# Batch 0's norms: rows summed on VectorE before one norm matmul a group, odd rows as two groups of 96 by 3

## The chip, the cores and the metric

The kernel runs on one core of a Trainium2 chip. The metric is device time in microseconds (us), median of several executions. One further execution was profiled; all lines shown of the profile are of that one.

## The reference

There are two parts, one after the other, over B = 4 batches of N = 6208 rows and C = 256 channels.

The first is an attention over channels. With q, k, v of shape (B, N, C):

```python
qn = q / (norm(q, axis=1) + 1e-6)      # one norm a batch and channel, over all N rows
kn = k / (norm(k, axis=1) + 1e-6)
s = kn.T @ qn / tau                    # (C, C) per batch
a = softmax(s, axis=-1)
x = v @ a                              # (N, C)
```

The second is a channel-mix network on x, with `x_prev` the row above:

```python
xk = mu_k * x + (1 - mu_k) * x_prev ;  xr = mu_r * x + (1 - mu_r) * x_prev
k = relu(xk @ w_k)                     # 256 -> 1024
out = sigmoid(xr @ w_r) * ((k * k) @ w_v)
```

So nothing of the output can be computed until all rows of a batch's q and k have been read. The sum of q times k gives the 256 by 256 matrix, and the sums of their squares over the rows give 512 norms.

## The kernel before

All instructions are written in the order in which each engine runs them; the schedule is fixed by the order of the calls. Semaphores make an instruction wait for the tiles it needs, and what stands behind it on the same engine waits with it.

**Batch 0** is loaded first, on its own. Rows come in groups: in the kernel before group 0 has the 64 odd rows (64 partitions, one row each), groups 1 to 11 have 128 partitions with four consecutive rows each, and groups 12 and 13 have 128 by 2. They are taken in the order 1, 2, 0, 3, ... 13. For each group the loop at lines 517 to 531 does this:

- `group_load` (line 121) issues two loads in float32 on SyncE's queue, one of q and one of k. At most eight loads of the queue are under way; a further one waits for the semaphore of an earlier one, and for its buffer.
- `group_cast` (line 138) makes bf16 copies of q and k on VectorE (line 142), and the squares of both, in bf16, on ScalarE (line 144).
- `unit_matmul` (line 171) adds the group's rows to the covariance in PSUM: two matmuls with 256 columns for each of the group's row slots (line 182), so eight for a group with four.
- `group_norms` (line 191) sums the squares over the partitions: a matmul with a block of ones as weights, one for each row slot, into one 32-partition strip of PSUM a slot (line 197). That is for groups up to `DIRECT` = 9.
- For the groups after it, 10 to 13, `norms_direct` (line 203) adds the sums into the final layout, with channels on partitions: four matmuls of one column for each row slot (line 210).
- `keep_warm(3)` (line 508) issues three matmuls whose result nobody reads, in groups 5 to 9.

At group 10 (`DIRECT + 1`), after its casts and before its matmuls, `copies` moves the strips from PSUM to SBUF on VectorE (line 224) and `gather` turns them into the final layout with four float32 matmuls (line 231; eight passes in the trace).

At group 11 a small copy on GpSimd (line 530) waits for the group's first cast. It holds back the loads on GpSimd's queue (v, the weights, batch 1's q and k) until then.

**The softmax of batch 0** then runs in a chain: `roots` on ScalarE (line 248, after a load of the function table), `evac` (264), `invert` on VectorE (256 to 259), `turn` on TensorE (271), `exp` (279), `weigh` (293), and `x_first` (364), with unread matmuls between them.

**The rest** is a loop over 48 blocks of 512 rows plus a last block, with the network of one block, the attention product of a later one and the covariance of batches 1 to 3 put between each other by hand. The v tiles must be transposed; from block 4 on a DMA on SyncE's queue does it (line 321), with the stores of the results (line 474) in the same queue. Norms of batches 1 to 3 are summed in another way (lines 163 to 169), which stays.

Of the kernel before, what the change touches and what calls it, by code (L numbers as in the profile page):

```python
# [14 lines left out]
OP = mybir.AluOpType  # L15
# [3 lines left out]
def kernel(  # L19
# [13 lines left out]
    nc = tc.nc  # L33
    B, N, C = q.shape
    D = C
    DF = moe_w_k.shape[1]
    P = 128
    M = 512
    S = M // P
    assert C == 256 and DF == 1024  # L40
    NB = N // M
    L = N - NB * M
# [16 lines left out]
    ones = const.tile([P, P], BF16, name="ones")  # L59
# [4 lines left out]
    thirty2 = const.tile([P, P], F32, name="thirty2")  # L64
# [21 lines left out]
    cov = {}  # L86
    bank = {}
# [2 lines left out]
    sums = {}  # L90
    now = [0]
    groups = {}
    summed = set()
    DIRECT = NB - 3

    def sizes(b):
        return [1] + [S] * (NB - 1) + ([S // 2] * 2 if b == 0 else [S])

    def order(b):
        g = list(range(len(sizes(b))))  # L100
        return [1, 2, 0] + g[3:]

    def rows_of(b, g):
        return (P if g else L), sizes(b)[g]

    def qk_src(t, b, g):
        if g == 0:
            return t[b, NB * M:, :].rearrange("(p j) c -> p j c", j=1)
        r = P * sum(sizes(b)[1:g])
        n = sizes(b)[g]  # L110
        return t[b, r:r + P * n, :].rearrange("(p j) c -> p j c", p=P)

    def apart(b, g):
        return b == 1 and g > 0
# [1 line left out]
    def rows_at(qk, b, g, i):  # L116
        if apart(b, g):
            return qk.rearrange("p s i c -> p (s i c)").rearrange("p (i s c) -> p i s c", i=2, s=S)[:, i]
        return qk[:, :, i]

    def group_load(b, g):
        rows, n = rows_of(b, g)
        qk = pq.tile([P, S, 2, C], BF16, name="qk", tag="qk", bufs=5)
        groups[b, g] = (qk,)
        if b == 0:
            qk2 = pq.tile([P, S, 2, C], BF16, name="qk2", tag="qk2", bufs=4)
            groups[b, g] += (qk2,)
            t_f = []
            for i, t in enumerate((q, k)):
                f = pq.tile([P, S, C], F32, name=f"f{i}", tag=f"f{i}", bufs=6)  # L130
                nc.sync.dma_start(f[:rows, :n], qk_src(t, b, g))
                t_f.append(f)
            groups[b, g] += tuple(t_f)
        else:
            for i, t in enumerate((q, k)):
                nc.gpsimd.dma_start(rows_at(qk, b, g, i)[:rows, :n], qk_src(t, b, g))  # L136

    def group_cast(b, g):
        rows, n = rows_of(b, g)
        qk, qk2, *t_f = groups[b, g]  # L140
        for i in range(2):
            nc.vector.tensor_copy(qk[:rows, :n, i, :], t_f[i][:rows, :n])  # L142
        for i in range(2):
            nc.scalar.activation(qk2[:rows, :n, i, :], t_f[i][:rows, :n], AF.Square)  # L144

    def unit_square(b, g, s):

        rows, n = rows_of(b, g)
        if s % 2:
            return  # L150
        qk = groups[b, g][0]
        if n == 1:
            t = pq.tile([P, 1, 2 * C], BF16, name="sq", tag="sq1", bufs=2)
            sums[b, "left"] = t
        elif (g, s) == (1, 0):
            t = pn.tile([P, 2, 2 * C], F32, name="acc", tag="acc", bufs=2)
            sums[b] = t
        else:
            t = pq.tile([P, 2, 2 * C], F32, name="sq2", tag=f"f{s // 2}", bufs=6)
            adds.append((now[0] + 2, b, t))  # L160
        if apart(b, g):
            for i in range(2):
                nc.scalar.activation(t[:rows, :, i * C:(i + 1) * C], rows_at(qk, b, g, i)[:rows, s:s + 2], AF.Square)
        else:
            nc.scalar.activation(t[:rows], qk[:rows, s:s + min(n, 2)].rearrange("p s i c -> p s (i c)"), AF.Square)  # L165
# [5 lines left out]
    def unit_matmul(b, g, s):  # L171
        rows, n = rows_of(b, g)
        t0 = g == order(b)[0] and s == 0
        te = g == len(sizes(b)) - 1 and s == n - 1
        if t0:

            cov[b] = (ps.tile([P, 2, C], F32, name="s_ps", tag="s_ps" if b else "vr_ps", bufs=1 if b else 2),
                      ps.tile([P, 2 * C], F32, name="ssq_ps", tag="vr_ps", bufs=2) if b == 0 else None)
        s_ps = cov[b][0] if b or g <= DIRECT else cov["s"]
        qk = groups[b, g][0]  # L180
        for ih in range(2):
            nc.tensor.matmul(s_ps[:, ih, :], rows_at(qk, b, g, 0)[:rows, s, ih * P:(ih + 1) * P],  # L182
                             rows_at(qk, b, g, 1)[:rows, s, :], start=t0 and ih == 0, stop=te,
                             skip_group_check=True)
        if s == n - 1 and b == 0:
            if g > DIRECT:
                norms_direct(g)
            else:
                group_norms(b, g)

    def group_norms(b, g):

        rows, n = rows_of(b, g)
        ssq_ps = cov[b][1]
        qk2 = groups[b, g][1]
        for u in range(n):
            nc.tensor.matmul(ssq_ps[32 * u:32 * (u + 1)], ones[:rows, :32],
                             qk2[:rows, u].rearrange("p i c -> p (i c)"),
                             start=u not in summed, stop=g == DIRECT, tile_position=(0, 32 * u),
                             skip_group_check=True)  # L200
            summed.add(u)

    def norms_direct(g):

        rows, n = rows_of(0, g)
        qk2 = groups[0, g][1]
        for u in range(n):
            flat = qk2[:rows, u].rearrange("p i c -> p (i c)")
            for i in range(4):
                nc.tensor.matmul(bank[0][:, C + i:C + i + 1], flat[:, i * P:(i + 1) * P], ones[:rows, 0:1],  # L210
                                 start=False, stop=g == len(sizes(0)) - 1 and u == n - 1, skip_group_check=True)

    def softmax_pieces(b):

        s_ps, ssq_ps = cov.pop(b) if b else cov[b]
# [5 lines left out]
        rk = rn[:, 2:4]  # L221
        def copies():
            cov["ssq"] = pn.tile([P, 2 * C], F32, name="ssq", tag="ssq", bufs=1)
            nc.vector.tensor_copy(cov["ssq"], ssq_ps)

        def gather():

            cov["s"] = cov[b][0]
            bank[b] = ps.tile([P, 2 * C], F32, name="bank", tag="xT_ps", bufs=2)
            for i in range(4):  # L230
                nc.tensor.matmul(bank[b][:, C + i:C + i + 1], cov["ssq"][:, i * P:(i + 1) * P], thirty2[:, 0:1],
                                 start=i == 0, stop=False, skip_group_check=True)

        def fold():
# [60 lines left out]
        if b == 0:  # L295
            return [copies, gather, roots, evac, invert, turn, exp, weigh_dve]
# [14 lines left out]
    def v_load(i):  # L311
        b, t = blocks[i]
        v_bf = p2.tile([P, S, C], BF16, name="v_bf", tag="v_bf", bufs=6)
        nc.gpsimd.dma_start(v_bf, v[b, t * M:(t + 1) * M, :].rearrange("(s p) c -> p s c", p=P))  # L314
        st[i, "v"] = v_bf
# [8 lines left out]
    def v_transpose_pe(i, evac):  # L324

        v_bf = st.pop((i, "v"))
        vT_ps = ps.tile([P, S, 2, P], BF16, name="vT_ps", tag="kT_ps", bufs=3)
        for s in range(S):
            for h in range(2):
                nc.tensor.transpose(vT_ps[:, s, h], v_bf[:, s, h * P:(h + 1) * P], ident)  # L330

        def go():
            vT = p2.tile([P, S, 2, P], BF16, name="vT", tag="vT", bufs=5)
            evac(vT, vT_ps)
            st[i, "vT"] = vT
        return go
# [171 lines left out]
    def keep_warm(n):  # L508

        junk_ps = ps.tile([P, M], F32, name="junk_ps", tag="kT_ps", bufs=3)  # L510
        for _ in range(n):
            nc.tensor.matmul(junk_ps, ones, fill, start=True, stop=True)

    mu_ps = ps.tile([P, 4], F32, name="mu_ps", tag="xT_ps", bufs=2)
    nc.tensor.transpose(mu_ps, mu_rows, ident_f[:4, :4])
    nc.vector.tensor_copy(mu_t, mu_ps)
    for g in order(0):
        group_load(0, g)
        group_cast(0, g)
        if g == DIRECT + 1:  # L520
            copies, gather, roots, evac, invert, turn, exp, weigh = softmax_pieces(0)
            copies()
            gather()
        for s in range(sizes(0)[g]):
            unit_matmul(0, g, s)
        if 5 <= g <= DIRECT:
            keep_warm(3)
        if g == NB - 1:

            nc.gpsimd.tensor_copy(gate, groups[0, g][0][:, 0, 0, 0:1])  # L530
            v_load(0)

    units = [(b, g, s) for b in range(1, B) for g in order(b) for s in range(sizes(b)[g])]
    loads = [(b, g) for b in range(1, B) for g in order(b)]
# [52 lines left out]
    go = v_transpose_pe(0, nc.vector.tensor_copy)  # L587
# [18 lines left out]
    for i in range(-2, NBLK - 1):  # L606
        for j in range(8):
# [26 lines left out]
            if i + 2 < NBLK:  # L634
                n = i + 2
# [78 lines left out]
```

## Time and profile before

| what | value |
|---|---|
| median of 6 runs | 513.28 us (512.68 to 514.12) |
| the profiled execution | time 514.12 us, span of its instructions 512.3 us |
| TensorE matmuls busy | 492.1 us, 96% of the span, 3524 instructions |
| VectorE busy | 440.9 us, 86% |
| ScalarE busy | 449.8 us, 88% |
| GpSimd busy | 99.9 us, 19% |
| 0 to 12.8 us: TensorE, VectorE, ScalarE busy | 4.81, 5.11, 7.13 us; 315 GB/s moved |
| 12.8 to 25.6 us | 11.79, 6.94, 10.57 us; 410 GB/s |
| 25.6 to 33 us | 5.45 of 7.4, 4.74, 6.16 us; 402 GB/s |
| 38 to 45 us | 5.94 of 7, 5.23, 3.89 us; 192 GB/s |
| 200 to 300 us | 99.94, 94.04, 94.26 us; 165 GB/s |

Busy time of a matmul is modelled, and matmuls overlap, so a full row doesn't mean that the array does its most. PE is TensorE, PEld its weight loads, DVE VectorE, ACT ScalarE, POOL GpSimd, SP SyncE. A group in the profile gives line, engine, operation, out<-in, shape and count, then busy us, mean ns of one, and the idle time before. In the timeline a row gives start and length in us, and neighbours of one kind are merged.

### The profile page before, as it was taken

Reading aid. Unit: us, or ns where it says so; the run is one execution under the profiler, and the core shown is the slowest. Engines: PE = TensorE matmul, PEld = TensorE weight load, DVE = VectorE, ACT = ScalarE, POOL = GpSimd, SP = SyncE. Lnnn points to the kernel's source line nnn. Section 1 sums busy time; section 2 is a strip of 40 time slices with the busy share of each in tenths; the row PEclk is TensorE's granted clock in tenths of the full one; section 3 lists DMA queues with packets and bytes.
Section 4 is the critical chain, followed back from the end, with each engine's and each line's share of the span. In section 5 each row is a group of like instructions: output and inputs, shape, how many; then the busy total and the mean of one; then the engine's idle time right before and its main releaser. Section 6 shows DMA issues by size and latency. Waiting matters only on the chain. (4 is left out here: it accounts for less than half of the span.)

```text
span 512.3 us, 9464 instructions
## 1 busy us (share of the span) xinstructions
PE 492.1 (96%) x3524; PEld 334.1 (65%) x3524; DVE 440.9 (86%) x725; ACT 449.8 (88%) x924; POOL 99.9 (19%) x146
## 2 busy tenths in 40 slices
PE   3988999999999999999999999999999999999996
PEld 2454666766676667667666667667666666666675
DVE  3567899998999999999989999999878787878884
ACT  5886999999899999999899999999897888878784
POOL 0044342223045123131243223000131100000000
PEclk9999999999999999999999999999999999999999
DMA  8999999999989999999499999925597573423123
GB/s 315 410 313 198 196 153 198 131 159 210 214 161 197 192 208 168 163 155 180 85 164 197 204 165 176 189 65 125 83 164 148 110 139 88 101 80 86 44 82 103
DMA packets 133462, 83.46 MB, mean 163 GB/s; under 512 B 50660, under 2 KB 126760, under 8 KB 133416
## 3 DMA queue, kind: packets, MB, share of 16 engines
q0 software_dynamic: 56592, 33.01, 49.7%
q1 hardware_dynamic: 76656, 49.72, 42.0%
q8 instruction: 27, 0.44, 0.4%
q10 hardware_dynamic: 168, 0.13, 0.1%
q14 instruction: 19, 0.16, 0.1%
HBM read 78.71 MB, written 25.43 MB: 203 GB/s over the span
## 5 line engine op out<-in xcount | busy, mean ns | idle before, releaser
L427 ACT ACTIVATE kr<-kT_ps 128x512 bf16<-128x512 f32 (+1 forms) x392 | 233.2, 606 | 28.7 <-PE kT_ps L422 24.8
L422 PE MATMUL kT_ps<-xk,w_k_sb 128*128 128x512 bf16 (+1 forms) x784 | 231.2, 377 | 0.4 <-DVE xk L407 0.2
L459 PE MATMUL vr_ps<-w_v_sb,kk 128*128 128x256 bf16 x1536 | 230.9, 273 | 0.2
L459 PEld LDWEIGHTS <-kk 128*128 128x128 bf16 x1536 | 149.7, 98 | 58.8 <-DVE kk L440 1.0
L469 DVE SCALAR_TENSOR_TENSOR res<-res,vr_ps 128x256 f32<-128x256 f32 x192 | 79.7, 415 | 44.5 <-ACT res L468 44.5
L440 DVE TENSOR_TENSOR kk<-kr 128x1536 bf16<-128x1536 bf16 (+2 forms) x148 | 116.7, 789 | 0.2 <-ACT kr L427 0.2
L422 PEld LDWEIGHTS <-w_k_sb 128*128 128x128 bf16 x784 | 75.9, 98 | 28.6 <-issue 1.2
L169 DVE TENSOR_TENSOR acc<-acc,sq 128x1024 f32<-128x1024 f32 x69 | 84.0, 1217 | 0.0
L182 PE MATMUL s_ps<-qk 128*128 128x256 bf16 x392 | 72.2, 284 | 6.0 <-DVE qk L142 5.7
L468 ACT ACTIVATE res<-vr_ps 128x256 f32<-128x256 f32 x192 | 76.4, 398 | 1.3 <-PE vr_ps L459 1.3
L455 PE MATMUL vr_ps<-w_r_sb,xr 128*128 128x256 bf16 x384 | 73.3, 272 | 1.1 <-DVE res L469 1.1
L407 DVE SCALAR_TENSOR_TENSOR xk<-delta,mu_t,xT 128x512 bf16<-128x512 bf16 x96 | 71.3, 745 | 0.0
L407 DVE SCALAR_TENSOR_TENSOR xr<-delta,mu_t,xT 128x512 bf16<-128x512 bf16 x96 | 71.2, 744 | 0.0
L455 PEld LDWEIGHTS <-xr 128*128 128x128 bf16 x384 | 37.5, 98 | 46.3 <-issue 2.5
L353 ACT CAST xT<-xT_ps 128x512 bf16<-128x512 f32 x94 | 55.3, 589 | 13.4 <-PE xT_ps L351 13.4
L351 PE MATMUL xT_ps<-vT,a_sb 128*128 128x512 bf16 x188 | 55.9, 379 | 2.3 <-DMA vT<-v_bf 2.0
L136 POOL DMA_DIRECT2D qk<-in_q_dram x39 | 26.3, 673 | 142.2 <-ACT kr L427 58.9
L165 ACT ACTIVATE sq<-qk 128x1024 f32<-128x1024 bf16 (+1 forms) x49 | 51.0, 1040 | 0.0
L182 PEld LDWEIGHTS <-qk 128*128 128x128 bf16 x392 | 38.9, 101 | 17.2 <-issue 8.0
L314 POOL DMA_DIRECT2D v_bf<-in_v_dram x48 | 37.3, 780 | 52.4 <-DMA vT<-v_bf 21.5
L397 DVE TENSOR_TENSOR delta<-xT 128x1024 bf16<-128x1024 bf16 x48 | 32.9, 685 | 1.9 <-ACT xT L353 1.8
L144 ACT ACTIVATE qk<-f 128x1024 bf16<-128x1024 f32 (+2 forms) x28 | 26.0, 948 | 7.7 <-DMA f<-in_q_dram 4.8
(82 smaller groups left out, 211.1 us busy)
## 6 DMA issues: line engine op xcount, KB each, us to landing
out_dram<-res SPq DMA_DIRECT2D x47, 512.0 KB, 4.2
v_bf<-in_v_dram POOLq DMA_DIRECT2D x48, 256.0 KB, 9.2
qk<-in_q_dram POOLq DMA_DIRECT2D x36, 256.0 KB, 7.8
qk<-in_k_dram POOLq DMA_DIRECT2D x36, 256.0 KB, 8.7
f<-in_q_dram SPq DMA_DIRECT2D x11, 512.0 KB, 8.8
f<-in_k_dram SPq DMA_DIRECT2D x11, 512.0 KB, 9.6
vT<-v_bf SPq DMA_TRANSPOSE x44, 8.8
f<-in_q_dram SPq DMA_DIRECT2D x2, 256.0 KB, 8.4
```

The costliest lines, as they stand in the source:

```text
L169: nc.vector.tensor_tensor(sums[b], sums[b], t, op=OP.add)
L182: nc.tensor.matmul(s_ps[:, ih, :], rows_at(qk, b, g, 0)[:rows, s, ih * P:(ih + 1) * P], rows_at(qk, b, g, 1)[:rows, s, :], start=t0 and ih ...
L351: nc.tensor.matmul(xT_ps, a_sb[:, b, ih, dh * P:(dh + 1) * P], vT[:, :, ih, :], start=ih == 0, stop=ih == 1)
L353: nc.scalar.copy(xT[:, dh, 1:], xT_ps)
L407: nc.vector.scalar_tensor_tensor(o[:, dh], st[i, "d"][:, dh], mu[:, dh:dh + 1], st[i, "x"][:, dh, :M], op0=OP.mult, op1=OP.add)
L422: nc.tensor.matmul(kT_ps[:, :m], w_k_sb[:, dh, fh * P:(fh + 1) * P], xk[:, dh, :m], start=dh == 0, stop=dh == 1)
L427: nc.scalar.activation(kr, kT_ps[:, :m], AF.Relu, scale=0.5 ** 0.5)
L440: nc.vector.tensor_tensor(st[i, "kk"][:, fh // 4 * 4 + lo:fh + 1, :m], kr, kr, op=OP.mult)
L455: nc.tensor.matmul(vr_ps[:, D:], xr[:, dh, s * P:(s + 1) * P], w_r_sb[:, dh, :], start=dh == 0, stop=dh == 1)
L459: nc.tensor.matmul(vr_ps[:, :D], kk[:, fh, s * P:(s + 1) * P], w_v_sb[:, fh, :], start=fh == 0, stop=fh == 7)
L468: nc.scalar.activation(res[:, s], vr_ps[:, D:], AF.Tanh, scale=0.5)
L469: nc.vector.scalar_tensor_tensor(res[:, s], res[:, s], 1.0, vr_ps[:, :D], op0=OP.add, op1=OP.mult)
```

## The change

The 64 odd rows and the first 512 are now taken together, as two groups of 96 partitions with three rows each (`W` = 96, `HEAD` = 3). So batch 0 has groups 0 and 1 with 96 by 3, groups 2 to 11 with 128 by 4, and 12 and 13 with 128 by 2, in plain order. `DIRECT` is now 10.

The squares of a group's row slots are added on VectorE, in place, in bf16: `row_sums` returns a first addition (the upper half onto the lower) and, for groups with more than two rows, a second. The loop hands them to the next group's `group_cast`, which runs one after each of its two casts. For the last group they follow the loop. `group_norms(g - 1)` comes one group later, after the next group's covariance matmuls, and has one matmul instead of one for each row slot (four instead of four for each slot after `DIRECT`).

`copies` and `gather` now come at group 11, behind its casts, the two additions in them, its eight covariance matmuls and the norm matmul of group 10. The copy takes 32 partitions instead of 128. `keep_warm(3)` is issued in groups 11 and 12 only, after the norms.

```diff
-    DIRECT = NB - 3
+    W = 3 * P // 4
+    HEAD = (M + L) // W // 2
+    DIRECT = NB - 2

     def sizes(b):
-        return [1] + [S] * (NB - 1) + ([S // 2] * 2 if b == 0 else [S])
+        return [HEAD] * 2 + [S] * (NB - 2) + [S // 2] * 2 if b == 0 else [1] + [S] * NB
...
     def rows_of(b, g):
+        if b == 0:
+            return (W if g < 2 else P), sizes(b)[g]
         return (P if g else L), sizes(b)[g]
...
-    def group_cast(b, g):
+    def group_cast(b, g, between):
         for i in range(2):
             nc.vector.tensor_copy(qk[:rows, :n, i, :], t_f[i][:rows, :n])
+            if between:
+                between.pop(0)()
...
+    def row_sums(g):
+        rows, n = rows_of(0, g)
+        qk2 = groups[0, g][1]
+        def first():
+            h = n // 2
+            nc.vector.tensor_tensor(qk2[:rows, :h], qk2[:rows, :h], qk2[:rows, h:2 * h], op=OP.add)
+        def second():
+            nc.vector.tensor_tensor(qk2[:rows, 0], qk2[:rows, 0], qk2[:rows, 1 if n == S else 2], op=OP.add)
+        return [first] + [second] * (n > 2)
...
-    def group_norms(b, g):
-        for u in range(n):
-            nc.tensor.matmul(ssq_ps[32 * u:32 * (u + 1)], ones[:rows, :32],
-                             qk2[:rows, u].rearrange("p i c -> p (i c)"),
-                             start=u not in summed, stop=g == DIRECT, tile_position=(0, 32 * u),
-                             skip_group_check=True)
-            summed.add(u)
-    def norms_direct(g):
-        for u in range(n):
-            flat = qk2[:rows, u].rearrange("p i c -> p (i c)")
-            for i in range(4):
-                nc.tensor.matmul(bank[0][:, C + i:C + i + 1], flat[:, i * P:(i + 1) * P], ones[:rows, 0:1], ...)
+    def group_norms(g):
+        rows, n = rows_of(0, g)
+        flat = groups[0, g][1][:rows, 0].rearrange("p i c -> p (i c)")
+        if g <= DIRECT:
+            nc.tensor.matmul(cov[0][1][:32], ones[:rows, :32], flat, start=g == 0, stop=g == DIRECT)
+            return
+        for i in range(4):
+            nc.tensor.matmul(bank[0][:, C + i:C + i + 1], flat[:, i * P:(i + 1) * P], ones[:rows, 0:1], ...)
...
+    LAST = len(sizes(0)) - 1
+    pending = []
     for g in order(0):
         group_load(0, g)
-        group_cast(0, g)
-        if g == DIRECT + 1:
+        group_cast(0, g, pending)
+        for s in range(sizes(0)[g]):
+            unit_matmul(0, g, s)
+        if g:
+            group_norms(g - 1)
+        if g - 1 == DIRECT:
             copies, gather, roots, evac, invert, turn, exp, weigh = softmax_pieces(0)
             copies()
             gather()
-        for s in range(sizes(0)[g]):
-            unit_matmul(0, g, s)
-        if 5 <= g <= DIRECT:
+        if DIRECT < g < LAST:
             keep_warm(3)
+        pending = row_sums(g)
...
+    for go in pending:
+        go()
+    group_norms(LAST)
```

More of the change, by code (lines that the diff above doesn't have):

```diff
@@ L92 @@
     groups = {}
-    summed = set()
-    DIRECT = NB - 3
+    W = 3 * P // 4
+    HEAD = (M + L) // W // 2
+    assert 2 * HEAD * W == M + L and HEAD <= S
+    DIRECT = NB - 2
     def sizes(b):
-        return [1] + [S] * (NB - 1) + ([S // 2] * 2 if b == 0 else [S])
+        return [HEAD] * 2 + [S] * (NB - 2) + [S // 2] * 2 if b == 0 else [1] + [S] * NB
     def order(b):
         g = list(range(len(sizes(b))))
-        return [1, 2, 0] + g[3:]
+        return [1, 2, 0] + g[3:] if b else g
     def rows_of(b, g):
+        if b == 0:
+            return (W if g < 2 else P), sizes(b)[g]
         return (P if g else L), sizes(b)[g]
     def qk_src(t, b, g):
-        if g == 0:
+        p, n = rows_of(b, g)
+        if b and g == 0:
             return t[b, NB * M:, :].rearrange("(p j) c -> p j c", j=1)
-        r = P * sum(sizes(b)[1:g])
-        n = sizes(b)[g]
-        return t[b, r:r + P * n, :].rearrange("(p j) c -> p j c", p=P)
+        r = sum(rows_of(b, h)[0] * rows_of(b, h)[1] for h in range(1 if b else 0, g))
+        return t[b, r:r + p * n, :].rearrange("(p j) c -> p j c", p=p)
     def apart(b, g):
@@ L178, in unit_matmul @@
                       ps.tile([P, 2 * C], F32, name="ssq_ps", tag="vr_ps", bufs=2) if b == 0 else None)
-        s_ps = cov[b][0] if b or g <= DIRECT else cov["s"]
+        s_ps = cov[b][0]
         qk = groups[b, g][0]
@@ L184, in unit_matmul @@
                              skip_group_check=True)
[L185 to L189, printed above, removed]
-    def group_norms(b, g):
-        rows, n = rows_of(b, g)
-        ssq_ps = cov[b][1]
-        qk2 = groups[b, g][1]
-        for u in range(n):
-            nc.tensor.matmul(ssq_ps[32 * u:32 * (u + 1)], ones[:rows, :32],
-                             qk2[:rows, u].rearrange("p i c -> p (i c)"),
-                             start=u not in summed, stop=g == DIRECT, tile_position=(0, 32 * u),
-                             skip_group_check=True)
-            summed.add(u)
-    def norms_direct(g):
-        rows, n = rows_of(0, g)
-        qk2 = groups[0, g][1]
-        for u in range(n):
-            flat = qk2[:rows, u].rearrange("p i c -> p (i c)")
-            for i in range(4):
-                nc.tensor.matmul(bank[0][:, C + i:C + i + 1], flat[:, i * P:(i + 1) * P], ones[:rows, 0:1],
-                                 start=False, stop=g == len(sizes(0)) - 1 and u == n - 1, skip_group_check=True)
+    def group_norms(g):
+        rows, n = rows_of(0, g)
+        flat = groups[0, g][1][:rows, 0].rearrange("p i c -> p (i c)")
[3 more added lines that the diff above has]
+        for i in range(4):
+            nc.tensor.matmul(bank[0][:, C + i:C + i + 1], flat[:, i * P:(i + 1) * P], ones[:rows, 0:1],
+                             start=False, stop=g == len(sizes(0)) - 1, skip_group_check=True)
     def softmax_pieces(b):
@@ L223, in copies @@
             cov["ssq"] = pn.tile([P, 2 * C], F32, name="ssq", tag="ssq", bufs=1)
-            nc.vector.tensor_copy(cov["ssq"], ssq_ps)
+            nc.vector.tensor_copy(cov["ssq"][:32], ssq_ps[:32])
         def gather():
-            cov["s"] = cov[b][0]
             bank[b] = ps.tile([P, 2 * C], F32, name="bank", tag="xT_ps", bufs=2)
             for i in range(4):
-                nc.tensor.matmul(bank[b][:, C + i:C + i + 1], cov["ssq"][:, i * P:(i + 1) * P], thirty2[:, 0:1],
+                nc.tensor.matmul(bank[b][:, C + i:C + i + 1], cov["ssq"][:32, i * P:(i + 1) * P], thirty2[:32, 0:1],
                                  start=i == 0, stop=False, skip_group_check=True)
```

## The prediction

> **What bounds the kernel now.** I read the page's chain first, then the timeline of the first 46 us, engine by engine, because every edit lies there; then the vector instructions by shape for prices; last TensorE's waits over the rest, to see whether a delay made early would still be there at the end.
>
> The chain, by engine and by line:
>
> ```profile
> PE 45%; DVE 0%; issue 0%; DVEq 0%
> PE vr_ps L459 18%; PE kT_ps L422 17%; PE vr_ps L455 4%; PE xT_ps L351 4%; PE s_ps L182 2%; PE y_ps L497 0%; PE st_ps L271 0%; PE r_ps L489 0%; DVE res L499 0%; PE bank L243 0%; PE xT_ps L385 0%; DVE xr L407 0%; DVEq L499 0%
> ```
>
> It is TensorE in the expert network. The change doesn't touch that, so it acts through the moment at which this part can begin. That is the end of batch 0's loading and of the short serial softmax after it.
>
> The timeline of the loading, three stretches of it (start, length, engine, line):
>
> ```profile
> 6.26 1.86 PE L182 MATMUL s_ps<-qk 128*128 128x256 bf16 x8 [1.97 <-DVE qk L142]
> ...
> 16.42 1.77 PE L182 MATMUL s_ps<-qk 128*128 128x256 bf16 x8
> ...
> 26.32 1.03 PE L182 MATMUL s_ps<-qk 128*128 128x256 bf16 x8 [0.44 <-DVE qk L142]
> ...
> 27.29 0.40 PE L197 MATMUL ssq_ps<-qk,ones 128*32 128x512 bf16 x4
> ...
> 27.62 0.82 PE L512 MATMUL junk_ps<-fill,ones 128*128 128x512 bf16 x3
> ```
>
> Eight covariance matmuls take 1.86 us until 16 us and 1.03 us from 18.6 us on: the array starts at half rate and changes once, near 18 us, after working nearly without a gap from 10.6 us. The matmuls at 23.76, 26.32 and 28.88 are 2.56 us apart: the loads' pace, 1 MiB in 2.56 us, 410 GB/s.
>
> The end of loading, on VectorE, ScalarE, TensorE in turn:
>
> ```profile
> 31.32 0.68 DVE L224 COPY ssq<-ssq_ps 128x512 f32<-128x512 f32 x1
> 32.07 0.69 DVE L142 CAST qk<-f 128x1024 bf16<-128x1024 f32 x1
> 33.30 3.08 DVE L142 CAST qk<-f 128x1024 bf16<-128x1024 f32 x5 [0.53 <-DMA f<-in_k_dram]
> ...
> 33.30 3.28 ACT L144 ACTIVATE qk<-f 128x1024 bf16<-128x1024 f32 x5 [0.15 <-DMA f<-in_k_dram]
> 36.59 1.28 ACT L248 ACT_TABLE_LOAD   x1
> 37.89 0.17 ACT L248 ACTIVATE rn<-bank 128x4 f32<-128x4 f32 x1
> ...
> 32.06 1.05 PE L231 MATMUL bank<-thirty,ssq 128*128 128x1 f32 x8 [1.07 <-DVE ssq L224]
> ...
> 36.87 0.34 PE L210 MATMUL bank<-ones,qk 128*128 128x1 bf16 x8
> ```
>
> The last group's k lands at 35.92, its square ends at 36.57, ScalarE loads the root's table, and the root runs at 37.89. The last norm matmul is done at 37.21, VectorE's last cast at 36.38: both hidden by the table load. So a delay of TensorE up to 0.68 us is free there, and everything above that moves the root.
>
> Prices, from the vector groups kept apart by shape, and one wait of TensorE between 45 us and the end:
>
> ```profile
> L440 DVE TENSOR_TENSOR kk<-kr 128x1024 bf16<-128x1024 bf16 x96 | 65.4, 682 | 0.2 <-ACT kr L427 0.2
> L440 DVE TENSOR_TENSOR kk<-kr 128x512 bf16<-128x512 bf16 x4 | 1.7, 418 | 0.0
> ```
>
> ```profile
> PE xT_ps L351 <- DMA vT<-v_bf: 2.0, 2, 1.1
> ```
>
> Those two waits stand at 104.10 (0.97 us) and 115.44 (1.06 us). They are for transposed v tiles that a DMA delivers; the queues are at work throughout 34 to 116 us. They are the only places where a later start could be made good.
>
> **What the Trainium skill says.** "TensorE: Matmul & The Clock Gate", section "What's actually happening": the array's clock is halved by default and freed only after a busy window of about 3.4 us. The trace agrees on the two rates (1.86 and 1.03 us); it needed 7 us of dense work here, and the stretch 11 to 14.5, filled about nine tenths, had not been enough. The page gives no threshold. The same page, "Architectural detail", has VectorE and ScalarE as strict first-in-first-out, so what stands behind a waiting instruction waits too. "VectorE: DVE Perf Modes", "What auto-detection actually checks", lets a two-source 16-bit operation run at twice the base rate; the 682 and 418 ns above are used instead of a formula.
>
> **The change, part by part.**
>
> *Loads.* Same bytes, 28 transfers as before; two of 64 KB disappear into four of 288 KB. The stream stays at 410 GB/s. In the trace 4 of 16 DMA engines appear to pause some 1.4 us around 8 to 9 us, just when the 1 KB rows pass; if they caused it, loading ends up to 1.4 us sooner. 1 KB packets took 46 ns against 159 for 4 KB, so they were no burden themselves. I take -0.2, bounds -1.4 to +0.5.
>
> *VectorE, middle groups.* A group gains an add of 1024 and one of 512: 0.68 + 0.42. With two casts of 0.69 that is 2.48 us of 2.56, and back-to-back instructions overlap by 0.08, so about 2.2. ScalarE's squares of the group before are done 0.2 us before its add. Nothing queues: zero, hidden by the loads. If the in-place add ran at half that speed, it would be 0.9 us a group over, for ten groups: excluded by the 682 ns row unless in-place differs.
>
> *TensorE, middle groups.* Four concurrent norm matmuls become one; both occupy 512 columns, so no time is freed at half rate. Fifteen fillers (5 x 0.65) leave groups 5 to 9. Time there is free, but the clock is not: at half rate a group streams 1.71 + 0.43 = 2.14 us of 2.56 (84%), at full rate 0.86 + 0.22 (42%). The 11 to 14.5 stretch was denser than 84% and didn't free the clock. So I expect it still halved, or back to half, at 34 us. I call this cold; the other outcome warm.
>
> *The tail, warm.* The sums' copy (L224) used to stand before the last whole group's casts and wait for nothing. It now stands behind that group's k cast and waits for its eight matmuls and the norm matmul of the group before. Queued behind it on VectorE are the four casts of the last two groups and four adds; behind those, all their matmuls. Cast ends 33.99; eight matmuls 0.95; norm 0.38; copy 35.4 to 36.1. Then VectorE: four casts (0.41 to 0.70 in this stretch, say 0.5 net), adds 0.60 and three of 0.34: 3.6, to 39.7. TensorE: gather 0.92 (32.06 to 32.98), three fillers 0.65, four matmuls 0.5, four norms 0.15, fillers 0.65, four matmuls 0.5, eight norms 0.34: 3.7, to 39.8. Root at about 40.0: +2.1.
>
> *The tail, cold.* Eight matmuls 1.80 (6.26 to 8.06), norm 0.61: copy 36.5 to 37.2. Then gather 1.4 (between 0.92 and twice that), fillers 1.3, matmuls 0.9, norms 0.25, fillers 1.3, matmuls 0.9, norms 0.5: 6.5, root at 43.75, +5.9. The fillers are dense from 38.6; if they free the clock by about 41, the last 2.9 us halve: +4.4. Middle +5.1. Further cold fillers in the softmax (two, two, six, seven) would add up to 1.5; I take 0.
>
> *Given back later.* Block transposes at 104 and 115 could absorb 0 to 2.0 us. The DMA queues work on while TensorE is late, but their later issues wait for buffers and result stores that the compute frees (the store of block 0 starts at 66.10, as soon as its data are there), so they shift too. I take half at most, -0.9.
>
> *Gate and weights.* The first v and weight loads start after the last whole group's q cast (32.77), which has nothing new to wait for: unchanged. First w_v use at 53.7, landed at 50.03: slack grows.
>
> Sum, cold: 5.1 - 0.2 - 0.9 = +4.0. The profiled execution has a span of 512.3 and a time of 514.12, 1.8 outside the span, 0.84 above the median of 513.28. On the median: 517.3.
>
> **Rivals.**
>
> 1. *Clock stays full.* For it: the page asks for one busy window, and 84% might do. Against it: 42% occupancy afterwards. Tail +2.1, less 0.2, less 0.5: +1.4, 514.7 (514.3 to 515.7).
> 2. *Warm, and the transposes' waits swallow the delay*: 513.3, within 0.8. For it: the DMA queues never go idle. Against it: the store at 66.10.
> 3. *Faster.* Without the 64 KB transfers the four DMA engines don't pause, all loads land 1.4 us sooner. That decides only if the clock is also full: +2.1 - 1.4 = +0.7, and the two waits return more than 1.7 of their 2.0, giving about 512.2. A measured end of loads before 34.6 us is the point where this begins.
> 4. *The copies' position costs nothing because VectorE catches up.* Excluded by the queue: after 34 us it has 4.6 us of work, where it had 2.3, and no loads left to hide it.
>
> **How the numbers follow.** Cold 0.50 (range 515.8 to 519.6, all slower); clock full with the delay left 0.28 (0.25 slower, 0.03 same); swallowed 0.14 (0.02 slower, 0.11 same, 0.01 faster); faster 0.08 (0.06 faster, 0.02 same). Slower 0.77, same 0.16, faster 0.07, where 0.2% (1.03 us) is about what a measurement tells from no change. Range 513.4 to 519.6: it leaves out the faster case and the lower half of the swallowed one.
>
> **What would show it.** Covariance matmuls of 1.8 us a set in the middle groups, and at 34 us: cold right. The copy starting at 36.5 (cold) or 35.4 (warm), casts of the last groups behind it, not at 34.05. Root at 42.3 to 43.8 or 40.0. VectorE with 0.3 us idle in a middle group. Last k landing at 35.9 or, against me, before 35. Waits for transposed v below 1 us in total: giving back right. A root before 38.6 makes the forecast wrong at its base; a root as forecast with a time within 1 us of before makes the giving-back term wrong.

## The result

The changed kernel takes 516.76 us in the median of 21 executions (513.80 to 518.12), the kernel before 513.18. The ratio is 1.0054, with a 95% interval of 1.0040 to 1.0067: slower, with an interval clear of no change. (This ratio is not that of the two medians, which would be 1.0070; it is close to that of the means, 516.11 to 513.37. The two differ because the times are not spread evenly.) The forecast was 517.3, in a range of 513.4 to 519.6.

One thing is needed to read this: the 21 times fall into two sets, 8 from 513.80 to 514.74 and 13 from 516.35 to 518.12. The mean clock granted to TensorE's array is on record for every execution, and it divides the sets without an overlap: 0.992 to 0.997 of full in the lower one, 0.986 to 0.990 in the upper. Since the clock is either full or half in all traces, that is an estimated 3 to 8 us at half rate in the one and 10 to 14 in the other (twice what is missing to 1, times the span; the start of the kernel, before the clock's first entry in the record, is not counted). In all eleven whole traces of this document the clock is full from 43.5 us to 510 us at least, so most of it falls into the head of the kernel: loading and softmax. The profiled execution took 514.73, so its trace shows the lower set only. An execution with a late softmax had to be caught in an experiment.

The chain of work that ended last runs through the same parts as before, the expert network's matmuls above all (the line numbers have moved):

```profile
PE vr_ps L461 18%; PE kT_ps L424 17%; PE vr_ps L457 4%; PE xT_ps L353 4%; PE s_ps L201 2%; PE y_ps L499 0%; PE st_ps L273 0%; PE r_ps L491 0%; DVE res L501 0%; PE bank L245 0%; PE xT_ps L387 0%; DVE xr L409 0%; DVEq L501 0%
```

The timeline of TensorE while batch 0 is loaded (start, length, engine, line; the middle groups):

```profile
16.63 1.03 PE L201 MATMUL s_ps<-qk 128*128 128x256 bf16 x8 [1.04 <-DVE qk L146]
17.59 0.39 PE L210 MATMUL ssq_ps<-qk,ones 128*32 128x512 bf16 x1
...
21.75 1.87 PE L201 MATMUL s_ps<-qk 128*128 128x256 bf16 x8 [1.21 <-DVE qk L146]
23.54 0.61 PE L210 MATMUL ssq_ps<-qk,ones 128*32 128x512 bf16 x1
```

The windows view of the same trace gives the granted clock; its columns are the stretch, its length, the busy time of PE, PEld, DVE, ACT and POOL with counts, PEclk, DMA share and GB/s:

```profile
14.00:18.00 4.00, 2.87 (x18) 1.71 (x18) 3.42 (x8) 3.27 (x4) 0.00 (x0) 1.00 1.03 410
18.00:22.00 4.00, 1.60 (x11) 1.13 (x12) 3.75 (x7) 3.39 (x4) 0.00 (x0) 0.91 1.03 410
22.00:26.00 4.00, 3.84 (x17) 2.01 (x15) 3.49 (x7) 3.23 (x4) 0.00 (x0) 0.50 1.03 410
26.00:30.00 4.00, 3.22 (x17) 1.84 (x17) 3.50 (x8) 3.17 (x3) 0.00 (x0) 0.74 1.03 410
30.00:34.00 4.00, 2.13 (x15) 1.22 (x13) 3.75 (x7) 3.37 (x4) 0.72 (x2) 1.00 1.02 396
34.00:38.00 4.00, 2.68 (x19) 1.94 (x19) 2.89 (x6) 3.98 (x6) 4.00 (x6) 1.00 0.97 198
```

By the clock's own record in the trace, the array goes full at 14.44 us, halves at 21.27, and is full again from 28.10: 6.83 us each. The loads run at 410 GB/s all the same.

The end of loading and the start of the softmax are called the tail; the root (`roots`, on ScalarE) is the first step of the softmax, and its start tells how late the softmax is.

The tail, on VectorE, ScalarE and TensorE in turn:

```profile
34.41 0.42 DVE L162 TENSOR_TENSOR qk<-qk 128x512 bf16<-128x512 bf16 x1
35.94 0.68 DVE L227 COPY ssq<-ssq_ps 32x512 f32<-32x512 f32 x1 [1.11 <-PE ssq_ps L210]
36.55 0.54 DVE L146 CAST qk<-f 128x512 bf16<-128x512 f32 x1
...
39.92 0.40 DVE L159 TENSOR_TENSOR qk<-qk 128x512 bf16<-128x512 bf16 x1
...
37.12 1.28 ACT L250 ACT_TABLE_LOAD   x1
40.86 0.17 ACT L250 ACTIVATE rn<-bank 128x4 f32<-128x4 f32 x1 [2.46 <-PE bank L213]
...
36.67 1.05 PE L233 MATMUL bank<-thirty,ssq 32*128 32x1 f32 x8 [0.77 <-DVE ssq L227]
...
40.48 0.34 PE L213 MATMUL bank<-ones,qk 128*128 128x1 bf16 x8
```

VectorE stands still for 1.11 us before the copy, and the casts of the last groups come behind it. The root, ready on ScalarE at 38.40, waits 2.46 us for the last narrow matmuls (those of one column). Before, it ran at 37.89 and waited for its own table. So the softmax starts 2.97 us later. Of this, about 0.5 is later loading: the last k lands at 36.45 instead of 35.92, and the k of group 11, on which the copy depends, is cast from 33.80 instead of 33.30. The other 2.44 to 2.47 come from the tail. The span is only 0.6 us longer. The waits of TensorE from 45 us to the end say why:

```profile
PE vr_ps L457 <- DVE res L471: 1.2, 2, 0.8
PE xT_ps L353 <- DVE vT L336: 0.2, 1, 0.2
```

The 2.0 us of waits for transposed v tiles have gone. From the root to the end it takes 472.1 us, where it took 474.5.

### The profile page after: what moved, and what is told of

Read it like the earlier page. It is cut to its first block, busy times and chain, and to the rows that moved or that the text cites. A ratio compares the mean times of both kernels' runs of the same rounds, so it can differ in the third digit from the quotient of the medians.

```text
span 513.0 us, 9352 instructions
## 1 busy us (share of the span) xinstructions
PE 490.7 (96%) x3455; PEld 333.4 (65%) x3455; DVE 453.2 (88%) x751; ACT 450.0 (88%) x924; POOL 99.8 (19%) x146
## 5 line engine op out<-in xcount | busy, mean ns | idle before, releaser
L201 PE MATMUL s_ps<-qk 128*128 128x256 bf16 (+1 forms) x394 | 73.4, 288 | 11.3 <-DVE qk L146 11.3
L201 PEld LDWEIGHTS <-qk 128*128 128x128 bf16 (+1 forms) x394 | 39.9, 102 | 23.5 <-issue 10.6
```

## The experiments

Two theories had to be told apart for the 3 us between the sets: the array's clock is half or full in the tail, by its own phase; or the spread comes from later transfers.

**The changed kernel again**, no edit.

> The changed kernel once more, unaltered, to see another execution's clock. Theory (halved array clock in the tail): the clock has windows of 3.41 us of its own phase; where the record shows it halved between 34 and 41 us, the root runs at 42.5 to 44 and the span is 515 to 516.5; where it is full there, the root runs at 40.9 and the span is 513 as in the profile at hand. Rival (the times spread by transfers in the second half): the span goes with the waits for transposed v tiles and the root stays at about 41 in any case.

Time 514.18, span 512.4, root at 40.42 though the last k landed at 37.42; the clock was half from 25.79 to 32.62 and full in the tail. No wait for transposed v. Both theories allow this; it shows that the phase of the clock moves from one execution to the next. It also shows which landing matters: the last k is 0.97 us later than in the first profile and the root is 0.44 us sooner, just as the k cast of group 11 is (33.36 against 33.80).

**Heads alone**: the kernel before, the changed one, and the changed one with more unread matmuls, each cut off after the first attention product. The edit, the same in all three:

```diff
-    next_load()
-    nc.gpsimd.dma_start(w_r_sb, ...)
-    v_load(2)
-    nc.gpsimd.dma_start(w_v_sb, ...)
-    v_load(3)
-    next_load()
...
-    keep_warm(7)
-    ... (the loop over the blocks and the last block)
+    end = const.tile([P, D], F32, name="end")
+    nc.vector.tensor_copy(end, st[0, "x"][:, 1, 1:1 + D])
+    nc.sync.dma_start(out[0, 0:P, :], end)
```

> The kernel before cut off after the first attention product: the 48 blocks, the last block and the loads that only they need are left out, and one tile is stored. A yardstick: its absolute time is about 47 to 49 us. Theory: its executions agree within 1 us, since its clock is full from 18 us on. Rival: they spread over 2 us or more, so that loading itself is the source of spread.

> The changed kernel cut off in the same way. Theory (halved clock in the tail in part of the executions): two sets of times, one 2.5 to 3.2 us over head_before, one 5 to 7.5 us over it, the second with about half of the executions. Rival (the spread of the changed kernel comes from later transfers): one set, within 1 us, about 3 us over head_before.

> The kernel fill_all (unread matmuls also in groups 5 to 10) cut off in the same way. Theory: only the lower set, 2.5 to 3.4 us over head_before, within 1 us, as the clock is held. Rival: the same spread as head_after.

Times: before 48.15 to 50.13 (4 executions), changed 50.05, 50.32, 50.47, 52.33, 53.48, 53.84, with more unread matmuls 50.46, 50.66, 50.85, 50.86, 52.30, 52.59. So the head spreads over 3.8 us and holds the whole gap between the two sets of the changed kernel: the rival that puts it later falls. The two sets lie less far above head_before's median of 49.18 than expected, 0.9 to 1.3 and 3.1 to 4.7 us. And head_before spreads over 2 us itself, which the theory had excluded: in its trace the clock halves at 32.79 and the root runs at 39.91. head_fill has two times in the upper region.

The clock on record sorts these times too. In head_after it is 0.912 to 0.930 for the three lower times and 0.860 to 0.863 for the three upper ones; in head_fill it is 0.999 or more for four and 0.966 for the two slow ones, which is one stretch of 3.4 us at half rate; in head_before it is 0.994 for the fastest and 0.910 for the slowest.

The profiled execution of head_after is one with the half clock. TensorE, then ScalarE:

```profile
34.12 1.67 PE L201 MATMUL s_ps<-qk 128*128 128x256 bf16 x8 [1.22 <-DVE qk L146]
35.72 0.61 PE L210 MATMUL ssq_ps<-qk,ones 128*32 128x512 bf16 x1
37.09 1.86 PE L233 MATMUL bank<-thirty,ssq 32*128 32x1 f32 x8 [0.77 <-DVE ssq L227]
...
43.67 0.17 ACT L250 ACTIVATE rn<-bank 128x4 f32<-128x4 f32 x1 [4.24 <-PE bank L213]
```

The clock was half from 34.36 to 44.60. VectorE's last addition ended at 39.98, so here TensorE sets the root, at 43.67. The last k had landed at 37.47. The repeat of the whole kernel is the twin of this trace: there the k of group 11 landed at 33.33 (33.35 here) and the last one at 37.42, but the clock was full in the tail:

```profile
40.42 0.17 ACT L250 ACTIVATE rn<-bank 128x4 f32<-128x4 f32 x1 [1.05 <-PE bank L213]
```

VectorE's last addition ended at 39.88 there, so landings and VectorE are alike within 0.1 us. With the half clock the root comes 3.25 us later, about the distance of the two sets (medians 514.15 and 517.49).

**More unread matmuls in the middle.**

```diff
-        if DIRECT < g < LAST:
+        if 5 <= g < LAST:
             keep_warm(3)
```

> The changed kernel with three unread matmuls also in groups 5 to 10. Theory: they hold the clock full from 18 us to the tail, the root always runs at about 40.9, and all times are at 513.8 to 514.7, median 514.2, 0.2% over the kernel before and 2.5 us under the changed one's median. Rival: the times still fall into two sets, with over half of them above 516, since the clock has nothing to do with it.

515.71 (6 executions, 514.92 to 517.03), ratio 1.0048, interval 1.0030 to 1.0067. In its trace the clock is full throughout from 12.74 and the root is at 41.27, but the median is not at 514.2, so it was measured once more:

> The kernel fill_all once more, unaltered, since its first run left only six times (514.92 to 517.03), among them two over 516.5. Theory (the upper times of the changed kernel are those with a halved clock in the tail): with the clock held, at most a tenth of the times lie more than 3.5 us over the median of the kernel before, and its ratio is 1.002 to 1.003. Rival (the clock explains little of the median, late loads or later transfers make the upper times): a third or more of the times lie that high, and the ratio is 1.0045 to 1.006, as that of the changed kernel.

516.58 (7 executions, 515.02 to 518.12), ratio 1.0069, interval 1.0044 to 1.0094. By its times the rival holds: four of seven lie over the bound, and the ratio is no better than the changed kernel's. The trace shows how the clock can be full all through the middle and be lost afterwards. Windows, then TensorE:

```profile
30.00:34.00 4.00, 2.79 (x15) 1.27 (x14) 2.34 (x5) 2.15 (x3) 0.16 (x1) 1.00 1.03 395
34.00:38.00 4.00, 2.09 (x16) 1.51 (x15) 2.88 (x6) 3.79 (x7) 4.00 (x7) 1.00 0.82 156
38.00:42.00 4.00, 4.00 (x20) 2.07 (x20) 2.91 (x7) 0.95 (x1) 3.09 (x4) 0.57 1.12 179
```

```profile
37.26 1.05 PE L233 MATMUL bank<-thirty,ssq 32*128 32x1 f32 x8 [0.77 <-DVE ssq L227]
38.24 1.45 PE L514 MATMUL junk_ps<-fill,ones 128*128 128x512 bf16 x3
```

From 34 to 38 us TensorE is busy for 2.09 of 4 us: it waits for the late loads, then for the copy, then does one-column matmuls. At 38.30 the clock halves, for 3.41 us; the root comes at 42.54. So putting the unread matmuls of the middle groups back does not make the changed kernel faster.

The clock on record says more than the times. In these 13 executions it is 0.992 to 1.0, and six have 0.998 or more; in the changed kernel it was never above 0.997, and 0.990 or less in 13 of 21. So those matmuls do hold the clock for longer. The six with a full clock take 514.92 to 515.88, the seven others 516.29 to 518.12: the clock still parts the times, against the rival's reason. But even the six are 2.0 to 3.0 us over the kernel before beside them. They are also above the changed kernel's lower set, and both traces have a late k of group 11, 3.18 and 4.00 us after that of group 10. So have the three other traces of the changed kernel's kind with unread matmuls in groups 5 to 10 (3.33 to 3.91); in the three without, it is 2.56 or 2.57. Whether the matmuls have to do with that is open. A late load also leaves TensorE idle, so in these executions the load and the clock can't be parted; the twin traces above can.

**The copy's wait alone**, on top of fill_all: the wide norms end at group 9, so that the copy, at the same place in VectorE's queue, finds its input long done.

```diff
-    DIRECT = NB - 2
+    DIRECT = NB - 3
...
         group_cast(0, g, pending)
+        if g == DIRECT + 2:
+            copies, gather, ... = softmax_pieces(0)
+            copies()
         for s in range(sizes(0)[g]):
             unit_matmul(0, g, s)
+        if g == DIRECT + 2:
+            gather()
         if g:
             group_norms(g - 1)
-        if g - 1 == DIRECT:
-            copies, gather, ... = softmax_pieces(0)
-            copies()
-            gather()
```

> As fill_all, but the last group summed by the wide norm matmul is 9, and the copy of the sums stands at the same place in VectorE's queue with nothing left to wait for (its norm matmul is a group old); group 10 goes to the four narrow matmuls. Theory (the copy's wait blocks VectorE): the copy starts at 34.75 instead of 35.94, and the root comes 0.9 to 1.2 us sooner than in fill_all, at 39.7 to 40.0; the time is 0.3 to 1.2 us lower. Rival (the additions and casts themselves, or TensorE's fillers, set the root): root within 0.3 us of fill_all's.

513.93 (22 executions), ratio 1.0029, interval 1.0016 to 1.0041; 1.8 us under fill_all's first run beside it. The 15 executions with a clock of 0.998 or more take 513.30 to 514.34, the seven others 514.83 to 517.22.

```profile
34.78 0.67 DVE L227 COPY ssq<-ssq_ps 32x512 f32<-32x512 f32 x1
35.38 0.44 DVE L146 CAST qk<-f 128x512 bf16<-128x512 f32 x1
...
39.29 0.17 ACT L250 ACTIVATE rn<-bank 128x4 f32<-128x4 f32 x1 [0.88 <-PE bank L213]
```

The copy starts as the queue reaches it. From the last landing to the root it takes 2.83 us, against 4.43 in fill_all and 1.97 in the kernel before; counted from the k cast of group 11 the difference to fill_all is the same. Both traces have a full clock. So the copy's wait is worth 1.6 us, the largest part of the tail's 2.44. More than expected (0.9 to 1.2), because the casts behind it also took 0.41 to 0.44 instead of 0.52 to 0.72. Why those casts vary is open.

**The unread matmuls of the tail**: copy_free without those of groups 11 and 12 (`if 5 <= g < NB - 1`).

> The kernel copy_free without the unread matmuls of groups 11 and 12 (those of 5 to 10 stay). In copy_free's trace the last covariance matmuls start at 38.48, right behind three of them, with their cast done at 38.10. Theory (these six cost only what they stand in the way): root 0.2 to 0.4 us sooner relative to the last landing, 513.3 to 513.8 in the median, 0.1 to 0.4 us under copy_free. Rival (without them the clock halves in the tail): root over 40.5 in the trace, median over 514.5.

514.48 (22 executions), ratio 1.0023, interval 1.0009 to 1.0037: not told apart from copy_free. In its trace the clock is half from 36.65 to 43.48, as the rival said; the root runs 3.10 us after the last landing, against 2.83 with them. The clock on record suggests that theory and rival are both right and cancel. Without these matmuls 7 of 22 executions have a clock of 0.998 or more, with them 15 of 22; but six of those seven take 512.78 to 513.34, less than all but one of the 15.

**The kernel before with late unread matmuls.**

```diff
-        if 5 <= g <= DIRECT:
+        if g in (NB - 1, NB):
             keep_warm(3)
```

> The kernel before with its unread matmuls in groups 11 and 12 instead of 5 to 9. Theory: without them the array's clock halves in a part of the executions (full for 6.8 us, half for 6.8 us, by its own phase); with the clock half in the tail the narrow norm matmuls end late and the root moves by 1 to 4 us; median 513.5 to 517, spread over 3 us. Rival (clock is held by the norm matmuls alone, or costs nothing in the tail): 513.2 within 0.5, spread as before.

515.27 (8 executions), ratio 1.0037, interval 1.0023 to 1.0051. As the theory had it: in the trace the clock is half from 29.27 to 39.51, and the root waits for TensorE until 42.74, 4.76 us after the last landing, where its own table was ready at 39.93:

```profile
38.65 1.28 ACT L248 ACT_TABLE_LOAD   x1
42.74 0.17 ACT L248 ACTIVATE rn<-bank 128x4 f32<-128x4 f32 x1 [2.81 <-PE bank L210]
```

All eight executions have a clock of 0.992 or less; of the 29 of the kernel before beside them, two have. So in the kernel before, the matmuls of the middle groups hold the clock, and with it the time. In the changed kernel they hold it too, but its tail leaves TensorE other gaps, and there putting them back gains nothing.

**The grouping alone**: the kernel before with the new `W`, `HEAD`, `sizes`, `order`, `rows_of` and `qk_src` for batch 0, and nothing else.

> The kernel before with the new row groups alone: two groups of 96 by 3 in plain order in place of the 64 odd rows; squares, norm matmuls per row slot, the copy at group 10 and the unread matmuls in 5 to 9 as before. Theory (the grouping moves the end of loading by under 0.3 us): last k lands at 35.9 to 36.3, or later only by a stall that other kernels show too; time 513.2 within 0.5, same. Rival (the grouping makes loading slower: 36.45 to 37.5 in the traces with it, against 35.9 to 36.05 in three of four without): time +0.5 to +1.0 us.

514.04 (22 executions), ratio 1.0025, interval 1.0012 to 1.0038. By its time the rival holds, but not by its reason. The first 3200 KB have landed at 12.3 to 13.5 us in five traces with the old groups and at 12.4 to 13.3 in nine with the new. The last k lands at 37.11 here, but at 37.33 in before_pe4, whose head has the old groups: in most of the traces, with either grouping, the last landings come 0.4 to 1.6 us behind the pace of the rest. The stream as a whole doesn't stand still then: from 14 to 34 us it moves 389 GB/s or more in every stretch of 4 us. What the new groups cost is open. In this trace the clock was half from 35.44 to 38.85, and it is 0.995 or less in 16 of the 22 executions, against 24 of 59 of the kernel before beside them.

**A later start alone**: the kernel before, with ten unread matmuls more ahead of the first attention product.

```diff
-    keep_warm(6)
+    keep_warm(16)
```

> The kernel before with ten more unread matmuls of 0.215 us in the softmax chain, ahead of the first attention product: a delay of 2.0 to 2.15 us of everything after it, and no other change. Theory (half is given back at the waits for transposed v tiles near 104 and 115 us): time +0.6 to +1.4 us, the two waits together below 1.2 us. Rival A (nothing is given back): +2.0 us, waits as before. Rival B (all is given back): within 0.4 us, the waits gone.

```profile
40.77 3.19 PE L512 MATMUL junk_ps<-fill,ones 128*128 128x512 bf16 x14
43.79 1.03 PE L364 MATMUL xT_ps<-vT,a_sb 128*128 128x512 bf16 x4
```

The product starts at 43.79 instead of 41.70, 2.09 us later. The time is 514.51, ratio 1.0026 (1.0018 to 1.0035), 1.3 us more: about 0.8 us is given back. In its trace the waits for transposed v are gone and the span, 512.5, is within 0.2 us of before's. The theory holds.

**One transpose less in the queue**: block 4's v tile by TensorE.

```diff
-            if (i, j) in ((-1, 5), (0, 4)):
+            if (i, j) in ((-1, 5), (0, 4), (1, 4)):
...
-            if j == 5 and 4 <= i + 5 < NBLK - 1:
+            if j == 5 and 5 <= i + 5 < NBLK - 1:
```

> The kernel before with the v tile of block 4 transposed on TensorE, as those of blocks 0 to 3 are, and not by a DMA: eight matmuls (0.61 us) and a copy on VectorE (0.68 us) more, one DMA transpose of a busy queue less. Theory (what a later start gives back lies in the transposes' DMAs being late): the waits near 104 and 115 us, 2.0 us in the kernel before, fall below 0.4; time -0.3 to -1.4 us. Rival (the waits move to other transposes, or VectorE is too full there): within 0.3 us or slower.

513.51 (22 executions), ratio 1.0014, interval 1.0002 to 1.0026: a miss. The waits are gone from its trace, but its loads ended at 37.33 and the clock was half from 34.27 to 37.68, with the root at 39.82, and a root that late removes these waits in any case. Whether it relieves the transposes is not told by this. By its time the rival (slower, or no gain) holds.

No version beat the kernel before.

## Why the prediction was right, and where it was not

The result lies in the range, 0.5 us under the forecast. That it is so close is in part luck. The forecast was a median on the assumption of a half clock in the tail, to which only 0.50 was given; the times are two sets 3.3 us apart, and the median fell into the upper one because 13 of 21 executions did. With ten or fewer there, it would have been 514.74 at most, the figure of rival 1. By its steps:

*Loads, -0.2.* Measured +0.53 in the profile, but equal heads differ by 1.4 us (35.92 and 37.33). The idea that the 64 KB transfers hold up four DMA engines fell with before_groups: without them the first 3200 KB came no sooner.

*VectorE, middle groups, hidden.* Right. The additions took 682 and 416 ns in place, and VectorE was idle for 0.26 us before the q casts of the profile. (At half that speed a group would have been about 0.7 us over its 2.56, by the same sum, not 0.9; that case didn't come about.) Not foreseen, and hidden too: the casts of the 96 by 3 groups took 943 ns, more than those of 128 by 4.

```profile
L146 DVE CAST qk<-f 128x1024 bf16<-128x1024 f32 x20 | 13.9, 693 | 2.4 <-DMA f<-in_q_dram 2.4
L159 DVE TENSOR_TENSOR qk<-qk 128x1024 bf16<-128x1024 bf16 x10 | 6.8, 682 | 0.0
L162 DVE TENSOR_TENSOR qk<-qk 128x512 bf16<-128x512 bf16 x10 | 4.2, 416 | 0.0
L146 DVE CAST qk<-f 96x768 bf16<-96x768 f32 x4 | 3.7, 943 | 1.3 <-DMA f<-in_q_dram 1.3
```

*TensorE, middle groups: the clock stays half, or falls back to half, by 34 us, since a denser stretch had not freed it; the unread matmuls no longer hold it.* Half of this step failed. The clock does not stay half: at half rate the groups' work freed it, and at full rate they lost it, 6.83 us full and 6.83 half in the profile, 10.24 and 6.83 in the repeat. The inference from the stretch of 11 to 14.5 us did not carry over: TensorE is busy throughout it in the trace of before and the clock stayed half, for a reason that is open, but in the middle groups of the changed kernel windows with 3.05 to 3.27 of 3.41 us busy freed it (after, again, head_after). So the tail's state is a matter of phase. The other half, that the clock goes because the unread matmuls are missing, fits the clocks on record (fill_all and before_late_fill). But it is not the whole reason: with these matmuls back in the middle (13 executions in two runs) the time was no lower, since the tail itself, with its wait for the copy, is late and can lose the clock as well, as at 38.30 in one trace.

*The tail, warm: root +2.1.* Measured 2.44 after the last landing. The copy started 1.45 us after the end of the k cast (34.49 to 35.94), where 1.4 was worked out; the whole was 0.3 short, and the casts behind it took up to 0.72 where 0.5 was taken.

*The tail, cold: root at 42.3 to 43.75.* head_after: 43.67, with the copy at 36.36 (36.5 forecast). The gather took 1.79 (1.4 taken, 0.92 to 1.84 given).

*Given back, -0.9.* About 0.8 of 2.09 in the median of before_delay, but 2.4 of 2.97 in the changed kernel's profiled execution, 2.0 of it the two waits that vanish. The profile of before, from which the forecast started, was 0.94 us above its median, so it may have had more of these waits to give than most executions have; that is not shown.

*Cold 0.50.* 13 of 21 times lie in the upper set, and these are the executions with the lowest clock (0.986 to 0.990). None of them was profiled whole, so that the half clock falls into the tail there rests on head_after and on a sum: where no wait for transposed v is left, the span was the root plus 471.9 to 472.5 us in six traces (after, again, fill_all, fill_all_again, copy_free, before_groups). A time of 517.4 less 1.8 outside the span then has its root near 43.5, which is head_after's.

*The rivals.* Clock full, 514.7: the lower set, 514.1, in whose two traces the clock is half in the middle and full in the tail. The transposes swallow the delay: in the lower set for the most part, 2.4 of 2.97 us in the profile. Faster: no execution. That VectorE catches up: no, as foreseen.

So the forecast had the right mechanism, a late copy in front of the last casts with a clock that is half in many executions. What it had wrong is that the clock would stay half, where it alternates and its phase decides, and that the missing unread matmuls would be the whole reason.

## What to carry to other kernels

An instruction that waits for another engine must not be queued ahead of work that is already due: here a 0.68 us copy moved by one group cost 1.6 us in the tail. In a stretch paced by loads the array's clock, which follows its own activity, can be half or full by phase, so one profile shows one of several kernels. Take several, or cut the stretch out and time it alone, and sort the times by the clock that is on record for each of them: here that parted two sets which the times alone left unexplained. A delay at the front is not all paid if a later wait has slack to give; find that wait first.

## What the runs showed that was not expected

- The array's clock changed only after multiples of about 3.41 us (3.41, 6.83, 10.24, 17.07, 20.48, 23.89), with a phase that differs between executions. The three traces without unread matmuls in the middle show where the bound lies there. A full clock was lost after a stretch of 3.41 us with 1.48 to 1.62 us of TensorE busy, and kept after one with 1.73 or more; a half one was freed after 3.05 to 3.27 busy, and not after 2.63 to 2.78. Four groups take 10.24 us, just three such stretches, so groups of equal work fill the stretches unequally. Busy time is only a rough measure of what the clock follows: in the tail of head_after, with its one-column matmuls, it stayed half after a stretch that was busy throughout, and head_fill kept a full clock after a stretch with 1.61 us.
- The kernel before is exposed as well: in the head of it the clock halved at 32.79 and the root came at 39.91, 2 us later than in its first profile.
- A cast of 96 by 768 (three row slots) took 943 ns, one of 128 by 1024 (four) 693 ns.
- The copy from PSUM took 0.68 us with 32 partitions as with 128.
